# Another order of the head, a band mask on VectorE, narrow blank matmuls and one stay for x, in an attention and gated-MLP kernel

## The chip, the cores and the metric

The kernel runs on one core of one Trainium2 chip. A core has TensorE (PE; its weight loads are a row of their own, PEld), VectorE (DVE), ScalarE (ACT), GpSimd (POOL), SyncE (SP, which issues DMAs) and 16 DMA engines. The metric is device time in microseconds of one execution; the time before is the median of three runs.

## The reference

Two stages, f32 in and out. Attention over 4 batches, 8 heads, 768 positions, 64 dimensions; each query sees the keys less than 16 positions away and one summary key for each block of 32 (the maximum of the block's keys, with the mean of its values):

```python
k_sum = k.reshape(B, H, nb, block, D).max(axis=3)
v_sum = v.reshape(B, H, nb, block, D).mean(axis=3)
mask_l = np.abs(pos[:, None] - pos[None, :]) < window
scores_s = scale * np.einsum('bhsd,bhnd->bhsn', q, k_sum) + np.log(block)
a = softmax(concat([np.where(mask_l, scores_l, -1e9), scores_s]))
x = a @ concat([v, v_sum])
...
h = x @ w_in                        # 3072 x 512 by 512 x 2048
g = h * (1.0 / (1.0 + np.exp(-beta * h)))
out = g @ w_out                     # by 2048 x 512
```

## The kernel before

**Tiles.** The four batches run one after the other. A batch has four pairs of heads, g = 0 to 3 (128 partitions hold two heads of 64), and two halves of 384 positions, u = 0 and 1. For each pair, `kT[g]` and `qn[g]` hold keys and queries turned by TensorE, `km[g]` the block maxima, `vst[g]` V as loaded (f32) and `ve[:, g]`, `vo[:, g]` its bf16 casts at two alignments. `e` is a pair's and half's exponentials, `xn` the attention result, `xT` the same turned, 4 x 128 rows, `h_sb` the gated MLP activations. PSUM is held as `one[0]`, `one[1]` (one bank each) and `big[0..2]` (two banks each); in the steps below a bank number x below 6 is half of `big[x // 2]`, 6 and 7 are `one[0]` and `one[1]`.

**The order.** All engines run in order of the program (the schedule is written by hand). Batch 0's first part is the list HEAD, one step for each entry: `kt`/`qt` turn k and q of a pair into a bank (16 transposes, L384), `kc`/`qc` copy them out on the engine named (a = ACT, d = DVE, p = POOL), `km` the block maxima, `vc` the cast of V, `vu`/`vl` copies from ve to vo, `sm`/`mc` the block means of V and their copy into `vm_one`, `sc` scores of (pair, half, big), `ex` their exponential on ACT, `av` the weighted sum of the first half, `no` its division (DVE), `xt`/`xc` the turn of x, `wi` a load of 512 columns of w_in, `begin` the first h matmuls, `blank` matmuls on zeros, `silu` the load of ScalarE's table.

**Scores.** In batch 0, `scores0` sums three things in PSUM: the summary keys (L415, 2 matmuls), the 96 keys around each tile of 64 queries (L422, 12 matmuls), and -30000 where the band ends, as matmuls of the identity with `off` (L417, 2 matmuls, 384 wide) and of `edge` (L426, 2 matmuls) at the first or last tile. Later batches instead multiply the exponentials by a 0/1 `mask` on DVE (`mask_e`, L451).

**After the head.** `main` holds TensorE's steps: eight `h_two` (two h tiles each of the first half, L578), sixteen `h_half` of the second half (L584), then output and the next batches. The table AT gives side steps a place in it: a step with place p follows main step number floor(p), so 1.99 stands behind the second h_two. Among them: `first` (`v_odd`, POOL copies, and `vm_rest`, four DVE copies of block means for two pairs, L480), `loads` (`more_loads`: k of batch 1, four parts of w_out, q of batch 1), `av0` (AV of the second halves of two pairs, 24 matmuls, and their norms), `x0` (x of the second halves of two pairs: six transposes and a DVE copy), `scale` (w_out by 1/beta on DVE, L337), `clear` (zeros in `kw` and `more_masks`, which makes `mask`), `kt` (k of batch 1).

**Queues of loads.** GpSimd issues the casting loads (f32 to bf16: k and q as rows, w_in, w_out) on one queue, in its own program order, between its casts and copies. SP issues V. `HOLD` puts V of pair 1 behind the third load of k, so pairs 1 to 3 of V start when k is in. In the head GpSimd's order is: loads of k and q, cast of V of pair 0, cast of pair 1 (it waits for that load), w_in part 0, two copies, w_in part 1, cast of pair 3 in two pieces, w_in parts 2 and 3.

Of the kernel before, what the change touches and what calls it, by code (L numbers as in the profile page):

```python
# [12 lines left out]
    'first': [-2.097, 0.853, -1.457, 0.459, 0.237, 1.035, 1.122, 1.113],  # L13
    'loads': [2.306],
    'av0': [1.99, 4.754],
    'x0': [5.759, 6.564],
    'scale': [8.171, 16.158, 16.833, 21.634],
    'clear': [6.428, 6.644],
# [84 lines left out]
def kernel(  # L103
# [190 lines left out]
    def more_masks():  # L294
        nc.vector.tensor_copy(out=mask[:], in_=band[:, None, :].to_broadcast([P, NT, QT]))
# [34 lines left out]
    def load_w_in(lo, hi):  # L330
        return nc.gpsimd.dma_start(out=w_in_sb[:, :, lo:hi], in_=w_in_r[:, :, lo:hi])
# [72 lines left out]
    def q_tile(g, h, m):  # L404
        return qn[g][h * D:(h + 1) * D, m * QT:(m + 1) * QT]
# [565 lines left out]
```

## Time and profile before

| | |
|---|---|
| three runs | 209.53, 209.86, 211.06 us; median 209.86 |
| the profiled execution | 210.59 us, span 208.9 us |
| TensorE, DVE, ACT, POOL busy | 96%, 66%, 60%, 29% of the span |
| first h matmul (L578) | 25.84 us |
| first h matmul of the second halves (L584) | 38.30 us |
| DMA queues | GpSimd's casting loads 22.0% of 16 engines' span, SP's and others' 54.9% and 8.8% |

The span runs from the first to the last instruction; the execution's own time has 1.69 us more around it. The chain of waits follows the last instruction back to what released it. A timeline's row has start, length, engine, line, operation, output and inputs, count, and in brackets the idle time before it with what ended it. Rows of several instructions overlap with their neighbours, since TensorE's matmuls are pipelined. A windows row gives the busy time of each engine within a stretch, then the clock granted to TensorE, the DMA engines' share and their GB/s.

### The profile page before, as it was taken

The page shows a single profiled execution, that of the slowest core. Times are in us where ns is not written, and L with a number is a line of the kernel's source. Part 1 is how long each engine was busy: PE and PEld are TensorE (multiplying, and loading weights), DVE is VectorE, ACT ScalarE, POOL GpSimd, SP SyncE. Part 2 cuts the span into 40 slices and gives each one's busy share as a digit, 9 for nine tenths or more (in the row PEclk, how much of TensorE's full clock was granted, in tenths as well). Part 3 has the DMA queues.
Part 4 walks back from the last instruction along what each step waited for, and adds up shares of the span by engine and source line. Part 5 has one row for each costly group of instructions (what it writes and reads, how often), then busy time and mean ns, then how long its engine had stood idle before and what let it go on. Part 6 is the DMA issues. An engine that isn't in the chain of part 4 may idle for free.

```text
span 208.9 us, 5772 instructions
## 1 busy us (share of the span) xinstructions
PE 200.0 (96%) x2383; PEld 138.9 (67%) x2387; DVE 138.8 (66%) x314; ACT 124.9 (60%) x189; POOL 61.5 (29%) x95
## 2 busy tenths in 40 slices
PE   7887899999999999999999999999999999999993
PEld 2476666665555675666888975667888856668882
DVE  4496674599999982868999621999889304464132
ACT  2365876679678212966979238768894439662210
POOL 7706991101530017422520162452501100000011
PEclk9999999999999999999999999999999999999998
DMA  5997999999958999999779979999936820000242
GB/s 114 188 221 124 167 208 207 206 207 222 184 139 222 218 246 260 225 188 209 148 173 250 199 213 285 205 192 202 122 126 66 189 100 3 0 0 3 100 100 100
DMA packets 79193, 34.12 MB, mean 163 GB/s; under 512 B 61488, under 2 KB 76224, under 8 KB 79168
## 3 DMA queue, kind: packets, MB, share of 16 engines
q1 hardware_dynamic: 61968, 23.92, 54.9%
q0 software_dynamic: 7424, 7.34, 22.0%
q10 hardware_dynamic: 9776, 2.50, 8.8%
q8 instruction: 18, 0.29, 0.6%
q14 instruction: 7, 0.06, 0.1%
HBM read 27.37 MB, written 6.29 MB: 161 GB/s over the span
## 4 chain that ended last, share of the span: by engine, by line
PE 78%; DMA 10%; DVE 6%; issue 2%; ACT 2%; POOL 1%; POOLq 0%
PE big L600 28%; PE one L664 16%; PE acc L664 12%; PE big L578 5%; DMA vst<-in_v_dram 4%; DMA w_in_sb<-in_moe_w_in_dram 4%; PE one L584 3%; DMA krow<-in_k_dram 3%; PE one L615 3%; PE one L600 2%; PE big L436 2%; PE big L511 2%; PE big L584 2%; PE big L384 1%; DVE xn L538 1%
## 5 line engine op out<-in xcount | busy, mean ns | idle before, releaser
L600 PE MATMUL big<-xT,w_in_sb 128*128 128x384 bf16 x360 | 60.5, 326 | 0.0
L600 PEld LDWEIGHTS <-w_in_sb 128*128 128x128 bf16 x384 | 37.6, 98 | 25.1 <-issue 0.7
L611 ACT ACTIVATE h_sb<-big,beta_sb 128x768 bf16<-128x768 f32 x45 | 39.6, 905 | 24.0 <-PE big L600 23.9
L664 PEld LDWEIGHTS <-h_sb 128*128 128x128 bf16 x320 | 30.6, 98 | 4.6 <-issue 0.2
L645 POOL TENSOR_TENSOR o_sb<-p,u 128x256 f32<-128x256 f32 x10 | 7.3, 728 | 84.8 <-DVE u L645 74.4
L447 ACT ACTIVATE e<-big,bias 128x768 bf16<-128x768 f32 x32 | 27.4, 900 | 6.7 <-PE big L426 4.3
L664 PE MATMUL one<-w_out_sb,h_sb 128*128 128x256 bf16 x240 | 30.4, 273 | 0.2 <-DVE u L645 0.2
L664 PEld LDWEIGHTS <-s_sb 128*128 128x128 bf16 x240 | 23.1, 98 | 3.3 <-issue 0.5
L645 DVE TENSOR_TENSOR s_sb<-h_sb 128x768 bf16<-128x768 bf16 (+2 forms) x16 | 7.8, 488 | 23.7 <-ACT h_sb L611 23.6
L645 DVE TENSOR_TENSOR u<-one,p 128x256 f32<-128x256 f32 x20 | 8.4, 419 | 17.4 <-PE one L664 17.4
L456 POOL CAST ve<-vst 128x832 bf16<-128x832 f32 (+2 forms) x16 | 14.5, 914 | 17.9 <-DMA vst<-in_v_dram 14.9
L615 PE MATMUL one<-w_out_sb,h_sb 128*128 128x512 bf16 x61 | 14.5, 380 | 0.4 <-issue 0.3
L451 DVE TENSOR_TENSOR e<-e,mask 128x768 bf16<-128x768 bf16 x24 | 14.1, 618 | 0.4 <-ACT e L447 0.2
L368 ACT COPY o_sb<-one 128x256 f32<-128x256 f32 (+1 forms) x14 | 6.1, 433 | 12.9 <-PE one L664 7.1
L365 POOL COPY kw<-km 128x288 bf16<-128x288 bf16 x12 | 6.4, 534 | 22.5 <-DVE km L357 12.2
L361 DVE TENSOR_REDUCE km<-kT 128x24 bf16<-128x768 bf16 x12 | 11.3, 944 | 2.1 <-ACT kT L368 2.1
L538 DVE TENSOR_TENSOR xn<-big,r 128x768 bf16<-128x768 f32 x12 | 11.5, 957 | 0.4
L578 PE MATMUL big<-xT,w_in_sb 128*128 128x384 bf16 x64 | 11.4, 326 | 0.3 <-DMA w_in_sb<-in_moe_w_in_dram 0.3
L664 PE MATMUL acc<-t_sb,h_sb 128*128 128x256 bf16 x80 | 10.9, 273 | 0.0
L368 ACT COPY p<-acc 128x256 f32<-128x256 f32 x10 | 3.8, 376 | 11.6 <-PE acc L664 7.3
L664 PE MATMUL one<-t_sb,s_sb 128*128 128x256 bf16 x80 | 10.4, 273 | 0.2 <-ACT o_sb L368 0.2
L831 ACT ACTIVATE h_sb<-big,beta_sb 128x384 bf16<-128x384 f32 x16 | 8.3, 578 | 3.7 <-PE big L578 3.7
(145 smaller groups left out, 315.0 us busy)
## 6 DMA issues: line engine op xcount, KB each, us to landing
out_dram<-o_sb SPq DMA_DIRECT2D x19, 256.0 KB, 3.5
vst<-in_v_dram SPq DMA_DIRECT2D x13, 336.0 KB, 5.2
kst<-in_k_dram SPq DMA_DIRECT2D x8, 384.0 KB, 4.8
qst<-in_q_dram SPq DMA_DIRECT2D x8, 384.0 KB, 4.5
w_in_sb<-in_moe_w_in_dram POOLq DMA_DIRECT2D x4, 512.0 KB, 8.9
w_out_sb<-in_moe_w_out_dram POOLq DMA_DIRECT2D x4, 512.0 KB, 14.2
vo<-ve SPq DMA_DIRECT2D x12, 107.2 KB, 2.6
vst<-in_v_dram SPq DMA_DIRECT2D x3, 416.0 KB, 8.9
```

The source lines that it names most:

```text
L361: nc.vector.tensor_reduce(out=km[g][:, NK:NK + nb], in_=kT[g][:, W:W + S].rearrange("p (n f) -> p n f", f=block), op=ALU.max, axis=AX.X)
L447: nc.scalar.activation(out=e[:], in_=s[:, :, 0:HS], func=ACTF.Exp, bias=bias[:, 0:1], scale=scale)
L451: nc.vector.tensor_mul(out=e.rearrange("p h (m q) -> p h m q", q=QT), in0=e.rearrange("p h (m q) -> p h m q", q=QT), in1=(mask2 if b > 1 e ...
L456: eng.tensor_copy(out=ve[:, g, lo:hi, 0:D], in_=vst[g][:, lo:hi])
L538: nc.vector.tensor_mul(out=x[:, 3 * us[0]:3 * us[0] + 3 * n].rearrange("p (k j) h d -> p k (j h) d", k=n), in0=tv[:, :, :, 0:D], in1=r[:, ...
L578: nc.tensor.matmul(t[:, 0:HS], w_in_sb[:, ki, i * P:(i + 1) * P], xT[:, ki, 0:HS], start=(ki == 0), stop=(ki == k1 - 1))
L584: nc.tensor.matmul(t[:, 0:HS], w_in_sb[:, ki, i * P:(i + 1) * P], xT[:, ki, lo:lo + HS], start=(ki == 0), stop=(ki == k1 - 1))
L600: nc.tensor.matmul(o, w_in_sb[:, ki, i * P:(i + 1) * P], x, start=(ki == 0), stop=(ki == k1 - 1))
L611: nc.scalar.activation(out=o, in_=t, func=ACTF.Silu, scale=beta_sb[:, i:i + 1])
L615: nc.tensor.matmul(t[:, 0:hi - lo], h_sb[:, n, ms * P:(ms + 1) * P], w_out_sb[:, n, lo:hi], start=(n == 0), stop=(n == k2 - 1))
L645: eng.tensor_tensor(out=o, in0=a, in1=b, op=op)
L664: nc.tensor.matmul(SLOTS[n], a[:, j, t * P:(t + 1) * P], b[:, j], start=(j == 0 and n not in (2, 3, 7)), stop=(j == J2 - 1), skip_group_ch ...
```

## The change

Five things change; the rest of the kernel and its arithmetic in later batches stay.

1. HEAD has another order, other banks and other engines for some copies. `blank` of 4 and of 2 matmuls, 512 wide, become 27 each of 64 wide (a single 512-wide one follows later). Both halves' scores of a pair stand near each other. `wi` 0 and 1 stand earlier in the list, and part 0 is issued as two loads of two 128-row chunks each.
2. The second halves' scores lose the `off` and `edge` matmuls; `mask_e(0, g, 1)` on DVE multiplies their exponentials by the mask instead, in four new side steps `mk0`.
3. For that, `more_masks` is a step of the head (`mask`), its row of ones moves from GpSimd's `mask` to DVE's `band`, and it leaves `clear`.
4. The side steps move: `av0` from 1.99 and 4.754 to 2.99 and 5.4, `vm_rest` of pairs 2 and 3 from about 1.1 to 3.5 and 3.6.
5. `x0` moves from 5.759 and 6.564 to 6.4 and 6.41: both turns of x behind the same h_two.

```diff
 AT = {
-    'first': [-2.097, 0.853, -1.457, 0.459, 0.237, 1.035, 1.122, 1.113],
+    'first': [-2.097, -1.9, -1.457, 0.459, 0.12, 0.13, 3.5, 3.6],
-    'av0': [1.99, 4.754],
-    'x0': [5.759, 6.564],
+    'av0': [2.99, 5.4],
+    'x0': [6.4, 6.41],
-    'clear': [6.428, 6.644],
+    'clear': [6.428],
+    'mk0': [0.2, 0.3, 3.7, 3.8],
...
 HEAD = [
-    ('blank', 10, 512), ('beta',), ('blank', 2, 512), ('kt', 0, 3), ('blank', 4, 512), ('kc', 0, 'a'), ('kt', 1, 6),
+    ('blank', 10, 512), ('beta',), ('blank', 2, 512), ('kt', 0, 3), ('blank', 27, 64), ('kc', 0, 'a'), ('kt', 1, 6),
...
+    ('sc', 2, 1, 1), ('wi', 2), ('ex', 2, 0), ('no', 1), ('vl', 3, 'd'), ('vl', 2, 'a'), ('mc', 2, 'a'), ('xt', 1, 5),
...
     def more_masks():
+        nc.vector.memset(band[NK:NK + nb], 1.0)
         nc.vector.tensor_copy(out=mask[:], in_=band[:, None, :].to_broadcast([P, NT, QT]))
...
-        nc.gpsimd.affine_select(out=mask[:, NT - 1], in_=mask[:, NT - 1], compare_op=ALU.is_ge, fill=0.0,
+        nc.gpsimd.affine_select(out=mask[0:NK, NT - 1], in_=mask[0:NK, NT - 1], compare_op=ALU.is_ge, fill=0.0,
                                 base=QT + W - 1, pattern=[[0, QT]], channel_multiplier=-1)
-        nc.gpsimd.memset(mask[NK:NK + nb], 1.0)
...
     def scores0(g, u, bg):
         s = big[bg]
+        edges = u == 0
...
-        for h, r in enumerate(H2):
+        for h, r in enumerate(H2 if edges else ()):
             nc.tensor.matmul(s[0:NK, h, 0:HS], off[r, h * QT:h * QT + NK],
...
-        for h, r in enumerate(H2):
+        for h, r in enumerate(H2 if edges else ()):
             c = u * (HT - 1) * QT
             nc.tensor.matmul(s[:, h, c:c + QT], edge[r, u], identity[r, r], start=False, stop=True)
...
     def w_in_part(i):
-        x = load_w_in(512 * i, 512 * i + 512)
+        x = load_w_in(512 * i, 512 * i + 512, 0, k1 // 2 if i == 0 else k1)
+        if i == 0:
+            load_w_in(0, 512, k1 // 2, k1)
...
-    at("clear", [clear_kw, more_masks])
+    at("clear", [clear_kw])
+    at("mk0", [lambda g=g: mask_e(0, g, 1) for g in range(G)])
```

GpSimd's queue in the head, from the cast of V of pair 1 (`vst1`) on. Before:

```order
L456 CAST ve_120<-vst1_92 128x13x64 [waits DMAHW3_49,Pool_49]
L331 DMA w_in_sb_183<-in_moe_w_in_dram 128x4x512 [waits DMASW0_49]
L374 COPY vo_121<-ve_120 32x2x3x64 [waits Pool_49]
L374 COPY vo_121<-ve_120 64x2x3x64
L331 DMA w_in_sb_183<-in_moe_w_in_dram 128x4x512
L456 CAST ve_120<-vst3_94 128x7x64 [waits DMAHW5_49,Pool_49]
L456 CAST ve_120<-vst3_94 128x6x64
```

After (lines of the changed kernel):

```order
L458 CAST ve_120<-vst1_92 128x13x64 [waits DMAHW3_49,Pool_49]
L332 DMA w_in_sb_183<-in_moe_w_in_dram 128x2x512 [waits DMASW0_49]
L332 DMA w_in_sb_183<-in_moe_w_in_dram 128x2x512
L332 DMA w_in_sb_183<-in_moe_w_in_dram 128x4x512
L458 CAST ve_120<-vst2_93 128x13x64 [waits DMAHW4_49]
L375 COPY vo_121<-ve_120 64x2x3x64 [waits Pool_49]
L458 CAST ve_120<-vst3_94 128x7x64 [waits DMAHW5_49,Pool_49]
```

The first load of w_in stands behind the same cast; the second now follows it with nothing between, and the cast of pair 2 has come to this queue (half of pair 3's has left it).

DVE's queue behind the head, from the copies of block means on (`e_415`, `e_474` are the second halves' exponentials of pairs 0 and 1, `r` and `xn` their norms). Before:

```order
L480 COPY ve_120<-vm_one_122 32x2x3x64
L537 RECIPROCAL r_725<-one0_78 128x6 [waits PE_49,Activation_49]
L538 TENSOR_TENSOR xn_420<-one0_78,r_725 128x384 [waits DVE_49]
L537 RECIPROCAL r_728<-one1_79 128x6 [waits PE_49]
L538 TENSOR_TENSOR xn_519<-one1_79,r_728 128x384 [waits DVE_49]
```

After:

```order
L482 COPY ve_120<-vm_one_122 32x2x3x64 [waits Pool_49]
L453 TENSOR_TENSOR e_415<-e_415,mask_111 128x768
L453 TENSOR_TENSOR e_474<-e_474,mask_111 128x768
L539 RECIPROCAL r_785<-one0_78 128x6 [waits PE_49,Activation_49]
L540 TENSOR_TENSOR xn_574<-one0_78,r_785 128x384 [waits DVE_49]
L539 RECIPROCAL r_788<-one1_79 128x6 [waits PE_49]
L540 TENSOR_TENSOR xn_630<-one1_79,r_788 128x384 [waits DVE_49]
```

Two masks stand between the copies of two pairs' means and the norms; the other two pairs' copies and masks follow behind these norms.

More of the change, by code (lines that the diff above doesn't have):

```diff
@@ L84 @@
 HEAD = [
[12 rows of a table removed]
[11 rows of a table added]
+    ('begin', 0, 2, 3), ('begin', 1, 0, 3), ('silu',),
 ]
@@ L329, with load_w_in @@
     w_out_r = moe_w_out.rearrange("(a p) n -> p a n", p=P)
-    def load_w_in(lo, hi):
-        return nc.gpsimd.dma_start(out=w_in_sb[:, :, lo:hi], in_=w_in_r[:, :, lo:hi])
+    def load_w_in(lo, hi, a=0, b=k1):
+        return nc.gpsimd.dma_start(out=w_in_sb[:, a:b, lo:hi], in_=w_in_r[:, a:b, lo:hi])
     def load_w_out(i, n=4):
@@ L412, in scores0 @@
         s = big[bg]
+        edges = u == 0
         H2 = [slice(h * D, (h + 1) * D) for h in range(2)]
         for h, r in enumerate(H2):
-            nc.tensor.matmul(s[:, h, 0:HS], km[g][r], qn[g][r, u * HS:(u + 1) * HS], start=True, stop=False)
-        for h, r in enumerate(H2):
+            nc.tensor.matmul(s[:, h, 0:HS], km[g][r], qn[g][r, u * HS:(u + 1) * HS], start=True, stop=not edges)
+        for h, r in enumerate(H2 if edges else ()):
             nc.tensor.matmul(s[0:NK, h, 0:HS], off[r, h * QT:h * QT + NK],
@@ L422, in scores0 @@
                 nc.tensor.matmul(s[0:NK, h, j * QT:(j + 1) * QT], kT[g][r, m * QT:m * QT + NK],
-                                 q_tile(g, h, m), start=False, stop=False)
-        for h, r in enumerate(H2):
+                                 q_tile(g, h, m), start=False, stop=not edges, skip_group_check=True)
+        for h, r in enumerate(H2 if edges else ()):
             c = u * (HT - 1) * QT
@@ L820 @@
             "qt": turn0("q", qrow), "qc": q_copy, "sm": means, "mc": means_copy, "sc": scores0,
-            "ex": lambda g, u: weigh(0, g, u), "vc": lambda g, e, lo=0, hi=JV: v_cast(eng_of(e), g, lo, hi),
+            "ex": lambda g, u: weigh(0, g, u), "mask": more_masks, "vc": lambda g, e, lo=0, hi=JV: v_cast(eng_of(e), g, lo, hi),
             "vu": upper, "vl": lower, "av": av0, "no": lambda g: norm(0, g, turns.pop(("o", g)), [0]),
```

20 rows, old and new, of the table HEAD are left out of this document.

## The prediction, made before the changed kernel ran

> **What bounds the kernel now.** I read the page's first part, then the chain of waits up to 80 us, then each engine's timeline over the first 40 us, and last the bytes that the DMA engines move in each microsecond there. Two lines of the page's first part first.
>
> ```profile
> span 208.9 us, 5772 instructions
> PE 200.0 (96%) x2383; PEld 138.9 (67%) x2387; DVE 138.8 (66%) x314; ACT 124.9 (60%) x189; POOL 61.5 (29%) x95
> ```
>
> TensorE has 8.9 us without work in the whole span, so a change of the head can win only what TensorE waits there, or what it does there for nothing. The chain of waits says what the head waits for (start, length, what):
>
> ```profile
> 3.36 6.06 DMA krow<-in_k_dram
> 9.44 7.76 DMA vst<-in_v_dram
> 17.32 0.82 POOL ve L456
> 18.14 7.65 DMA w_in_sb<-in_moe_w_in_dram
> 25.84 0.82 PE big L578 x4
> ...
> 38.46 0.65 PE one L584 x4
> ...
> 58.51 0.91 ACT e L447
> ...
> 59.44 1.58 DVE e L451 x2
> ```
>
> So the head isn't TensorE's: k's third row load ends, the load of V of pair 1 held behind it lands, GpSimd casts that, and only then issues w_in, whose first part lands at 25.8. The first h matmul (L578) starts on it. From there TensorE is almost never idle. But DVE is full as well, from 39.85 on:
>
> ```profile
> 39.85 1.14 DVE L337 TENSOR_SCALAR w_out_sb<-w_out_sb,inv_beta 128x512 bf16<-128x512 bf16 x4 [1.68 <-DMA w_out_sb<-in_moe_w_out_dram]
> ...
> 39.90:58.00 18.10, 18.03 (x205) 10.38 (x204) 18.07 (x33) 13.90 (x23) 3.85 (x7) 1.00 1.15 204
> 58.00:76.00 18.00, 17.29 (x276) 10.88 (x278) 17.07 (x33) 9.11 (x15) 1.87 (x2) 1.00 0.98 191
> ```
>
> The windows' numbers are length, then busy time of PE, PEld, DVE, ACT and POOL, then clock, DMA share and GB/s. Between 39.90 and 58.00 TensorE works 18.03 of 18.10 us and DVE 18.07. DVE's row of work starts when the first part of w_out lands (its 1.68 us of waiting say so) and runs into the masks of batch 1 at 59.44. Hence two chains must both become earlier: TensorE's, from the first h matmul, and the DMA stream that ends in w_out. The end moves by the smaller of the two gains.
>
> **The change part by part.** GpSimd's issues first.
>
> ```profile
> 17.32 0.88 POOL L456 CAST ve<-vst 128x832 bf16<-128x832 f32 x1 [7.95 <-DMA vst<-in_v_dram]
> 18.14 0.76 POOL L331 DMA_DIRECT2D w_in_sb<-in_moe_w_in_dram  x1
> 18.94 1.05 POOL L374 COPY vo<-ve 32x384 bf16<-32x384 bf16 x2
> 19.93 0.74 POOL L331 DMA_DIRECT2D w_in_sb<-in_moe_w_in_dram  x1
> 20.72 1.01 POOL L456 CAST ve<-vst 128x448 bf16<-128x448 f32 x2
> 21.67 1.48 POOL L331 DMA_DIRECT2D w_in_sb<-in_moe_w_in_dram  x2
> ```
>
> In the list of steps w_in moves far ahead, but on GpSimd's queue the cast of pair 1 still stands before it, and what that cast waits for (vst at 17.2) isn't touched: the first issue stays at 18.14. After it come three issues in a row (two halves of part 0, then part 1): 18.14 + 3 x 0.75 = 20.4, then the cast of pair 2 (0.88, until now on DVE), a 0.50 copy and half of pair 3's cast (0.50): 22.3. The last two parts follow at 22.3 and 23.0 instead of 21.67 and 22.4; the stream has work until then (two parts of 512 KB at some 200 GB/s, from 20.25 to 25.4). The mask's select on GpSimd and pair 0's copy (0.50) run in its 7.95 us of waiting: nothing.
>
> What the stream can win stands in its windows:
>
> ```profile
> 20.00:21.00 1.00, 0.98 (x23) 0.73 (x23) 0.85 (x3) 0.98 (x3) 0.96 (x2) 1.00 0.69 109
> 22.00:23.00 1.00, 0.87 (x30) 0.73 (x27) 0.32 (x2) 0.95 (x2) 1.00 (x2) 1.00 1.25 179
> 23.00:24.00 1.00, 0.74 (x20) 0.63 (x21) 0.80 (x4) 0.82 (x2) 0.90 (x3) 1.00 0.81 74
> 24.00:25.00 1.00, 1.00 (x32) 0.83 (x30) 0.71 (x2) 0.33 (x1) 0.90 (x3) 1.00 1.13 181
> 40.00:45.00 5.00, 5.00 (x59) 3.11 (x58) 5.00 (x11) 3.07 (x7) 0.00 (x0) 1.00 1.25 210
> ```
>
> Against the 205 to 210 GB/s of the full stream, 22 to 25 us lack 26 + 131 + 24 of 205, or 0.9 us: a hole between the first part of w_in and the second, which was issued 1.8 us after it. Issued 0.75 us after the one before it, the second should close it. I take 0.75 us (the ends: 0.9, and below nothing 0.75 lost, if every transfer on this queue pays such a start and there is now one more). Then w_out's first part lands near 39.1, and DVE's row starts 0.75 earlier.
>
> TensorE's chain. A score step shows what the second halves lose (first rows of the pieces of one step):
>
> ```profile
> 18.80 0.34 PE L415 MATMUL big<-qn,km 64*128 64x384 bf16 x2
> 18.97 0.33 PE L417 MATMUL big<-identity,off 64*96 64x384 bf16 x2
> 19.14 0.42 PE L422 MATMUL big<-qn,kT 64*96 64x64 bf16 x12
> 19.39 0.19 PE L426 MATMUL big<-identity,edge 64*128 64x64 bf16 x2
> 19.52 0.27 PE L519 MATMUL one<-vm_one,e 128*128 128x65 bf16 x3
> ...
> 17.50 0.23 PE L422 MATMUL big<-qn,kT 64*96 64x64 bf16 x2 [1.32 <-issue]
> ...
> 22.30 0.57 PE L473 MATMUL one<-ve,A_avg 128*32 128x128 bf16 x14
> ...
> 14.87 0.36 PE L519 MATMUL one<-vm_one,e 128*128 128x65 bf16 x6
> 15.16 0.22 PE L525 MATMUL one<-ve,e 96*64 96x65 bf16 x1
> ```
>
> The step takes 0.72; without L417 (0.17) and L426 (0.13) 0.42. Four such steps: 1.2 us of TensorE gone, but most of it in a stage that waits for vst anyway (1.32 us of standing up to 17.50). What counts is the tail behind the sums of pairs 2 and 3, which need pair 3's cast: 22.30 now, 22.3 then. Behind them come sums 0.57, scores 0.42, x 0.17, AV 0.60, x 0.17, AV 0.60 and x 0.17, together 2.70, with about 0.3 of waits for DVE's norm of pair 2 as the last x needs it: the first h matmuls at 25.3 instead of 25.84. Part 0's first half, 256 of 512 KB, is there by then: 1.3 us less to move at 200 GB/s, so 24.5 where the whole part lands at 25.8. So 0.55 us.
>
> Behind that nothing is added to TensorE: the same 64 matmuls L578, 48 of AV, 12 transposes of x. Moving the second halves' x into one stay saves at most the small waits; 0 taken, 0.3 as the upper end. AV of the second halves now waits for the masks. Their price:
>
> ```profile
> 57.70 3.32 DVE L451 TENSOR_TENSOR e<-e,mask 128x768 bf16<-128x768 bf16 x4
> ...
> 65.77 1.03 DVE L451 TENSOR_TENSOR e<-e,mask 128x768 bf16<-128x768 bf16 x2
> ...
> 27.32 0.35 DVE L480 COPY vo<-vm_one 32x384 bf16<-32x384 bf16 x1
> ...
> 29.23 0.25 DVE L480 COPY ve<-vm_one 32x384 bf16<-32x384 bf16 x1
> ```
>
> A mask costs 0.52 to 0.83. DVE is done with the norms at 25.9; four of the eight copies of the means (27.32 to 29.48 now, so 1.1 for four) and two masks (1.0 to 1.7) end by 28.7, and AV of pairs 0 and 1, one h tile later than before, starts at 29.4. The second two masks end near 33.7, AV of pairs 2 and 3 starts at 33.9: just covered, 0.1 lost at worst; without the cover each mask costs TensorE its full 0.8. The mask's making (0.35, from 37.67 to the head) lies before kc of pairs 2 and 3, while TensorE waits for vst anyway: nothing.
>
> The 54 narrow blanks: the 128-row, 65-wide matmuls L519 follow each other at 0.048 us (six between 14.87 and 15.16), so 27 take 1.3 us against 0.97 and 0.4 of four and two wide ones. The transposes of k for pairs 1 to 3 come 0.3 to 0.5 later; 5 us lie between them and the wait for vst: nothing.
>
> The sum: TensorE 0.55 earlier, the stream 0.75 earlier, so the end 0.55 earlier. The profiled execution took 210.59 us with a span of 208.9; it gives 210.04. It lay 0.73 above the median of 209.86, to which I apply the same 0.55: 209.3 us.
>
> **The rivals.** The hole stays. DVE works from 19.30 to 20.32 on a cast between SBUF tiles while GpSimd writes the second part's request (19.93), and in the new order DVE copies V of pair 1 (19.1 to 20.0) beside the issue at 19.6. If such DVE work holds the request back, the hole is there again, w_out lands at 39.85 as before, and DVE's full row takes back what TensorE won: 209.8. Against it: the four issues last 740 to 759 ns alike, beside DVE or not. The Trainium skill, page "SBUF — State Buffer", section "Who interferes with whom", says that a DVE copy between SBUF tiles in a two-port mode locks GpSimd out, so that a GpSimd DMA starves for descriptors; the equal durations neither show it nor exclude it, and by that rule the sum is this rival's.
>
> One more start. The split makes five transfers of four. If the hole is a price of each start on a queue that has little in it, there are two holes of 0.75, one more than now: w_out lands at 40.6 and DVE's full row starts as much later: 210.6, slower. For it: the hole has the form of the first start (20 to 21 us, 109 GB/s). Against it: no later boundary in the stream shows one.
>
> A cold TensorE. Its work thins out: from 17 to 22.3 us stand sums 0.5, scores 0.42 and 0.72 and AV 0.6, or 2.2 us, where there were 3.6 (sums, three whole score steps, AV, two x), and the wide blanks become narrow.
>
> ```profile
> 1.27 4.45 PE L737 MATMUL one<-blank 128*128 128x512 bf16 x10 [1.27 <-DVE blank L232]
> 7.09 1.04 PE L737 MATMUL one<-blank 128*128 128x512 bf16 x4
> 16.00:17.00 1.00, 0.18 (x8) 0.11 (x5) 1.00 (x2) 0.00 (x0) 0.00 (x0) 1.00 1.27 237
> ```
>
> The first ten blanks took 0.44 each, later ones 0.24: about 4.4 us at half speed until it runs fast. Should that come again when h begins, 4.4 us of matmuls cost 2.2 more: 211.5. It decides only if the thin stage counts as idle; the 1.3 us of standing at 16 to 17 us did not slow the matmuls behind it. The Trainium skill, "TensorE: Matmul & The Clock Gate", section "HAM oscillation — how this bites in real kernels", asks for a gap of about 3.4 us; no single gap here is half of that, so its rule lowers this rival's chance.
>
> **How the numbers follow.** My forecast (the hole closes) has 0.48, its own range 208.9 to 209.7. The hole stays: 0.28. One more start: 0.12. Cold TensorE: 0.05. The rest, 0.07, is a gain beyond the forecast, with the full 0.85 of stream and waits or more. I take 208.4 to 210.8, which holds the first three and the spread of the runs before, and leaves out the cold case and both ends. A measurement of this kernel tells about 1% (2.1 us) from no change; every case but the cold one and part of the rest lies within it: faster 0.05, same 0.88, slower 0.07.
>
> **What would show it.** The hole: no microsecond from 21 to 26 under 150 GB/s, and the wait of DVE for w_out ending near 39.1. TensorE: first h matmul at 25.3, first L584 matmul (second halves) near 37.8. Masks: no wait of AV for the masks over 0.2. I am wrong if the first issue of w_in moves from 18.14, if TensorE's matmuls in h are spaced by more than 0.17, or if DVE's row between 40 and 58 shortens although nothing in it is changed.

## The result, and the profile after

The changed kernel takes 211.01 us (median of 20 runs, 209.91 to 212.49), the kernel before 209.98 (median of 20 runs, 209.01 to 211.83). The ratio is 1.0051, with a 95% interval of 1.0031 to 1.0071: 0.5% slower and just above the range of 208.4 to 210.8, where a gain of 0.55 us was forecast. The profiled execution took 211.23 us with a span of 209.4 (before: 210.59 and 208.9).

First the chain of waits of the changed kernel, from the landing of k to batch 1 (start, length, what):

```profile
10.37 6.24 DMA vst<-in_v_dram
16.73 0.88 POOL ve L458
17.61 2.12 POOL w_in_sb L332 x3
19.73 0.89 POOL ve L458
20.69 0.58 POOL vo L375
21.33 0.57 POOL ve L458
21.94 0.55 PE one L475 x13
25.40 1.28 PE big L580 x4
27.00 3.43 PE big L580 x20
...
38.81 0.65 PE one L586 x4
...
59.85 1.63 DVE e L453 x2
...
83.73 15.76 PE big L602 x96
```

Before, the chain went from the cast of V of pair 1 through the landing of w_in to the first h matmuls (L578). Now it goes through GpSimd's own row: the cast, three requests (2.12 us), two more casts with a copy between them, and then TensorE's sums of pairs 2 and 3 (L475). The h matmuls (now L580) begin earlier, at 25.19 instead of 25.84; of that 0.59 us is an earlier landing of V in this execution (its cast starts at 16.73 instead of 17.32). But the first four take 1.28 us, where four took 0.65 elsewhere, and the h matmuls of the second halves (now L586) come at 38.81 instead of 38.46, the second pair of masks of batch 1 at 59.85 instead of 59.44, the 96 h matmuls of batch 1 (now L602) at 83.73 instead of 83.16. Hence 0.35 of the 0.57 us seen at 83.73 has arisen by 40 us.

TensorE's clock in single microseconds (third number from the end; it was 1.00 in each of these microseconds before), and, from TensorE's timeline, what stood ahead:

```profile
21.00:22.00 1.00, 0.06 (x3) 0.06 (x4) 0.64 (x3) 0.42 (x1) 0.94 (x3) 1.00 1.23 191
23.00:24.00 1.00, 1.00 (x27) 0.91 (x26) 0.53 (x2) 0.97 (x2) 0.90 (x3) 0.91 1.15 185
24.00:25.00 1.00, 1.00 (x22) 0.84 (x20) 0.58 (x2) 0.48 (x1) 0.93 (x2) 0.50 1.20 196
27.00:28.00 1.00, 1.00 (x7) 0.56 (x6) 0.97 (x3) 0.95 (x2) 0.94 (x2) 0.88 1.24 209
```

```profile
20.69 0.23 PE L475 MATMUL one<-ve,A_avg 128*32 128x128 bf16 x1 [0.33 <-DVE xn L540]
21.94 0.55 PE L475 MATMUL one<-ve,A_avg 128*32 128x128 bf16 x13 [1.02 <-POOL ve L458]
```

TensorE waits 0.33 us for the norm of pair 0 and 1.02 for GpSimd's cast of pair 3. It works 0.06 of the microsecond at 21. Two us later its clock is half, until 27.2: 3.4 us, in which about 1.7 us of work is lost.

The loads, in longer stretches (the last number is GB/s), before and then after:

```profile
20.00:24.00 4.00, 3.59 (x88) 2.86 (x88) 2.90 (x9) 3.72 (x6) 3.85 (x7) 1.00 0.98 139
30.00:37.00 7.00, 7.00 (x74) 4.47 (x71) 3.28 (x20) 4.84 (x11) 2.05 (x3) 1.00 1.24 207
```

```profile
20.00:24.00 4.00, 2.65 (x67) 2.12 (x66) 2.76 (x9) 2.81 (x6) 3.77 (x7) 0.98 1.11 161
30.00:37.00 7.00, 7.00 (x89) 4.34 (x88) 4.77 (x14) 5.13 (x11) 2.69 (x4) 1.00 1.13 171
```

The hole at 23 to 24 us is gone, but 20 to 24 us move 161 GB/s, not 205, and a second hole has opened: 30 to 37 us move 171 instead of 207. That costs 7 x 36 / 207 = 1.2 us of the full stream. What is loaded there was requested later, by GpSimd's timeline (before at 27.51 and 28.29), and w_out lands hardly sooner than before, by DVE's:

```profile
27.46 0.72 POOL L466 COPY vo<-ve 32x384 bf16<-32x384 bf16 x1
28.13 0.79 POOL L196 DMA_DIRECT2D krow<-in_k_dram  x1
28.91 2.99 POOL L335 DMA_DIRECT2D w_out_sb<-in_moe_w_out_dram  x4
```

```profile
27.07 1.52 DVE L453 TENSOR_TENSOR e<-e,mask 128x768 bf16<-128x768 bf16 x2
33.32 1.03 DVE L453 TENSOR_TENSOR e<-e,mask 128x768 bf16<-128x768 bf16 x2
39.72 1.14 DVE L338 TENSOR_SCALAR w_out_sb<-w_out_sb,inv_beta 128x512 bf16<-128x512 bf16 x4 [1.13 <-DMA w_out_sb<-in_moe_w_out_dram]
```

So there were three suspects, all of them new: the half clock, the masks on DVE (two pairs at 27.07 and 33.32, beside the loads that thin out), and the requests (w_in's part 0 in two, k and w_out later).

### The profile page after: what moved, and what is told of

Same layout as the page of the kernel before. It is cut to its first block, busy times and chain, and to the rows that moved or that the text cites. A ratio compares the mean times of both kernels' runs of the same rounds, so it can differ in the third digit from the quotient of the medians.

```text
span 209.4 us, 5848 instructions
## 1 busy us (share of the span) xinstructions
PE 201.4 (96%) x2420; PEld 140.2 (67%) x2420; DVE 139.9 (67%) x318; ACT 124.9 (60%) x191; POOL 63.7 (30%) x94
## 4 chain that ended last, share of the span: by engine, by line
PE 81%; DMA 6%; DVE 5%; POOL 3%; ACT 2%; issue 1%; ACTq 0%; POOLq 0%; DVEq 0%
PE big L602 28%; PE one L666 17%; PE acc L666 13%; PE big L580 5%; PE one L586 3%; DMA krow<-in_k_dram 3%; DMA vst<-in_v_dram 3%; PE one L617 3%; PE one L602 2%; PE big L438 2%; PE big L513 2%; PE big L586 2%; PE big L385 2%; DVE e L453 1%; ACT e L449 1%
## 5 line engine op out<-in xcount | busy, mean ns | idle before, releaser
L602 PE MATMUL big<-xT,w_in_sb 128*128 128x384 bf16 x360 | 60.5, 326 | 0.0
L602 PEld LDWEIGHTS <-w_in_sb 128*128 128x128 bf16 x384 | 37.6, 98 | 25.0 <-issue 0.7
L449 ACT ACTIVATE e<-big,bias 128x768 bf16<-128x768 f32 x32 | 27.2, 899 | 3.3 <-PE big L438 1.2
L647 DVE TENSOR_TENSOR s_sb<-h_sb 128x768 bf16<-128x768 bf16 (+2 forms) x16 | 8.8, 553 | 24.0 <-ACT h_sb L613 24.0
L458 POOL CAST ve<-vst 128x832 bf16<-128x832 f32 (+1 forms) x16 | 14.4, 908 | 13.1 <-DMA vst<-in_v_dram 7.9
L453 DVE TENSOR_TENSOR e<-e,mask 128x768 bf16<-128x768 bf16 x28 | 17.0, 635 | 1.3 <-ACT e L449 1.0
L366 POOL COPY kw<-km 128x288 bf16<-128x288 bf16 x12 | 7.4, 620 | 28.5 <-DVE km L358 18.6
L617 PE MATMUL one<-w_out_sb,h_sb 128*128 128x512 bf16 x64 | 15.0, 380 | 0.0
L540 DVE TENSOR_TENSOR xn<-big,r 128x768 bf16<-128x768 f32 (+1 forms) x13 | 12.0, 927 | 0.4
L580 PE MATMUL big<-xT,w_in_sb 128*128 128x384 bf16 x64 | 12.1, 343 | 0.0
L570 POOL CAST qn<-qst 128x768 bf16<-128x768 f32 x8 | 8.2, 1034 | 9.9 <-DMA qst<-in_q_dram 5.9
L666 PE MATMUL acc<-t_sb,s_sb 128*128 128x256 bf16 x80 | 10.4, 273 | 0.0
```

The costliest lines, as they stand in the source:

```text
L449: nc.scalar.activation(out=e[:], in_=s[:, :, 0:HS], func=ACTF.Exp, bias=bias[:, 0:1], scale=scale)
L453: nc.vector.tensor_mul(out=e.rearrange("p h (m q) -> p h m q", q=QT), in0=e.rearrange("p h (m q) -> p h m q", q=QT), in1=(mask2 if b > 1 e ...
L458: eng.tensor_copy(out=ve[:, g, lo:hi, 0:D], in_=vst[g][:, lo:hi])
L540: nc.vector.tensor_mul(out=x[:, 3 * us[0]:3 * us[0] + 3 * n].rearrange("p (k j) h d -> p k (j h) d", k=n), in0=tv[:, :, :, 0:D], in1=r[:, ...
L580: nc.tensor.matmul(t[:, 0:HS], w_in_sb[:, ki, i * P:(i + 1) * P], xT[:, ki, 0:HS], start=(ki == 0), stop=(ki == k1 - 1))
L602: nc.tensor.matmul(o, w_in_sb[:, ki, i * P:(i + 1) * P], x, start=(ki == 0), stop=(ki == k1 - 1))
```

## The experiments

In what follows the stream is the row of GpSimd's casting loads, and the dip is its thin stretch from 30 to 37 us.

All are the changed kernel or the kernel before with one or two edits. Each was run 12 times beside the kernel before, whose medians were 210.06, 210.14, 210.24 and 210.20 in the four groups of four. The column "20 to 24" and "30 to 37" are the loads' GB/s in the profiled execution, "asked" the start of the request for k of batch 1, "h, half 2" the first h matmul of the second halves there.

| run | median us | ratio to before, 95% interval | 20 to 24 | asked | 30 to 37 | h, half 2 |
|---|---|---|---|---|---|---|
| before (20 runs) | 209.98 | 1 | 139 | 27.51 | 207 | 38.30 |
| changed (20 runs) | 211.01 | 1.0051 [1.0031, 1.0071] | 161 | 28.13 | 171 | 38.64 |
| fill | 211.26 | 1.0052 [1.0021, 1.0084] | 139 | 28.11 | 177 | 37.35 |
| v3first | 211.11 | 1.0046 [1.0010, 1.0082] | 177 | 28.01 | 173 | 36.44 |
| nomask | 210.30 | 1.0018 [0.9988, 1.0048] | 133 | 27.64 | 203 | 37.30 |
| oldhead | 210.67 | 1.0025 [0.9990, 1.0061] | 158 | 26.37 | 202 | 37.18 |
| early | 210.10 | 0.9996 [0.9966, 1.0025] | 168 | 25.18 | 206 | 38.48 |
| nomask_late | 210.92 | 1.0053 [1.0026, 1.0079] | 160 | 28.42 | 181 | 36.84 |
| v3early | 209.93 | 0.9988 [0.9959, 1.0018] | 164 | 24.94 | 206 | 36.60 |
| row | 209.95 | 1.0001 [0.9972, 1.0029] | 206 | 26.61 | 176 | 37.55 |
| after_early | 210.68 | 1.0025 [0.9995, 1.0055] | 172 | 24.95 | 206 | 38.10 |
| v3early_whole | 209.40 | 0.9979 [0.9951, 1.0007] | 206 | 24.48 | 205 | 37.22 |
| row_early | 210.19 | 1.0012 [0.9987, 1.0036] | 204 | 24.22 | 203 | 37.84 |
| row_split | 210.46 | 1.0021 [0.9991, 1.0050] | 167 | 26.29 | 207 | 37.34 |
| after_whole | 209.83 | 0.9973 [0.9942, 1.0005] | 204 | 26.84 | 177 | 37.11 |
| after_early_whole | 209.37 | 0.9950 [0.9920, 0.9980] | 208 | 24.49 | 202 | 36.63 |
| early_whole | 209.99 | 0.9978 [0.9945, 1.0011] | 205 | 24.09 | 204 | 36.83 |
| v3_noblank | 210.18 | 0.9971 [0.9934, 1.0007] | 207 | 24.66 | 205 | 38.90 |

The ratio is an estimate with its interval and not the quotient of the two medians; in v3_noblank, whose runs fall into two clusters, they differ most. A difference of two medians under some 0.5 us is not told apart by 12 runs; the columns of the profile are each of one execution. When the load of V of pair 1 lands moves them too: its cast began between 15.31 and 17.32 us, for no reason that an edit gives.

### First group: clock or masks

`fill`, blanks in TensorE's wait:

```diff
-('sm', 7, 2, 3),
+('blank', 5, 512), ('sm', 7, 2, 3),
```

> The changed kernel with five 512-wide blank matmuls where TensorE stands from 20.7 to 21.9 us, before the sums of pairs 2 and 3. Cold theory (the standing makes the clock fall to half for 3.4 us, and that is what costs): clock 1.00 from 20 to 30 us, first h matmul near 24.7 instead of 25.4, first h matmul of the second halves near 37.5 instead of 38.8, median 0.8 to 1.3 us under the changed kernel's 211.0, so 209.7 to 210.2. Stream theory (the loads that end in w_out and DVE's row behind them set the end, and the clock costs nothing there): clock 1.00 too, but w_out lands near 39.7 as before and the median stays at 210.8 to 211.2.

Measured: 211.26 us, clock 1.00 from 20 to 40 us, the second halves' h at 37.35, 1.3 us earlier than in the changed kernel. But w_out lands at 40.11, and TensorE loses what it had won (windows of fill, then DVE's row):

```profile
40.00:58.00 18.00, 16.60 (x197) 9.64 (x195) 17.59 (x33) 13.03 (x22) 5.06 (x6) 1.00 1.17 200
```

```profile
40.11 1.14 DVE L338 TENSOR_SCALAR w_out_sb<-w_out_sb,inv_beta 128x512 bf16<-128x512 bf16 x4 [2.82 <-DMA w_out_sb<-in_moe_w_out_dram]
```

TensorE works 16.60 of 18 us from 40 to 58, where it was full (17.93) before; 1.4 us of that is one wait for q of batch 1, the last of the casting loads. The cold theory falls as an account of the end: with the clock repaired the loads take the gain back.

`v3first`, pair 3's cast before pair 2's copy on GpSimd:

```diff
-('sc', 1, 1, 1), ('vu', 2, 'p'), ('ex', 1, 0),
+('sc', 1, 1, 1), ('ex', 1, 0),
...
-('vc', 3, 'p', 0, 7),
+('vc', 3, 'p', 0, 7), ('vu', 2, 'p'),
```

> The changed kernel with GpSimd's cast of V of pair 3 ahead of its copy for pair 2: the sums of pairs 2 and 3 can start near 21.3 instead of 21.9, and TensorE stands about 1.0 instead of 1.6 us. Cold theory: if 1.0 us is short enough, the clock stays at 1.00 and h begins 1.3 us earlier, median 209.5 to 210.0; if not, the clock still falls for 3.4 us, h begins 0.6 earlier and the median is 210.4. Stream theory: no change at the end, 210.8 to 211.2.

Measured: 211.11. The second halves' h at 36.44 is 1.9 us earlier than in the kernel before, and the end isn't: ahead of the turn of q of batch 1, at 51.15 us, TensorE waits 1.3 us for DVE's scaling of w_out, whose first part landed only at 39.59. The stream theory's number.

`nomask`, the mask back on TensorE:

```diff
-        edges = u == 0
+        edges = True
...
-    at("mk0", [lambda g=g: mask_e(0, g, 1) for g in range(G)])
```

> The changed kernel with the mask of the second halves back on TensorE (the matmuls of off and edge for both halves) and no masks on DVE. Mask theory (the masks on DVE slow the loads beside them, 30 to 37 us at 131 to 185 GB/s, and with them w_out): no dip there, w_out lands near 38.6, median 210.0. Cold theory: the clock falls as in the changed kernel, up to 0.3 us more TensorE work ahead of h, median 211.0 to 211.5.

Measured: 210.30, no dip, w_out at 39.02. This fits the mask theory. But there is another difference: k was requested at 27.64, not 28.13, and the loads were further behind (133 GB/s from 20 to 24 us). Of these 0.49 us, 0.32 come from an earlier V load and at most 0.17 from copies on GpSimd that no mask holds up. The half clock is missing from this profile as well, so nomask alone doesn't separate the three suspects.

`oldhead`, the kernel before's HEAD in the changed kernel:

```diff
 HEAD = [
-    ('blank', 10, 512), ('beta',), ('blank', 2, 512), ('kt', 0, 3), ('blank', 27, 64), ('kc', 0, 'a'), ('kt', 1, 6),
+    ('blank', 10, 512), ('beta',), ('blank', 2, 512), ('kt', 0, 3), ('blank', 4, 512), ('kc', 0, 'a'), ('kt', 1, 6),
...
-    ('kc', 1, 'a'), ('blank', 27, 64), ('km', 0), ('kt', 2, 5), ('vc', 0, 'p'), ('kt', 3, 0), ('km', 1), ('mask',),
+    ('kc', 1, 'a'), ('blank', 2, 512), ('km', 0), ('km', 1), ('mask',), ('vc', 0, 'p'), ('vl', 0, 'p'), ('kt', 2, 7), ('kc', 2, 'd'),
```

> The changed kernel with the list HEAD of the kernel before (only the mask's making added to it; the wide blanks are back too, since they stand in the list), all else as changed: masks on DVE, side steps at their new places, w_in part 0 in two loads. Cold theory: clock 1.00 throughout the head, first h matmul near 25.5, median 209.5 to 210.0, at or under the kernel before. If the side steps, the masks or the split load are to blame: 210.8 to 211.3 at clock 1.00.

Measured: 210.67, between the two, and its clock was half from 11.6 to 15.0 us, in another place. Masks on DVE and no deep dip: against the mask theory. It left open what is slow in it; the split, below, is one part that it shares with the changed kernel.

### Second group: when the loads are requested

What separates the profiles with a dip from those without is how late k was asked for, seen from where the stream stood. `early` is fill with the requests moved and nothing else:

```diff
-    'loads': [2.306],
+    'loads': [-1.8],
```

> The run with five blanks (fill) and one thing more: k of batch 1, the four parts of w_out and q of batch 1 are requested before GpSimd's copies of pairs 2 and 3, so near 25.6 us instead of 28.1; the masks stay on DVE. Late-request theory (the stream runs dry at 30 to 37 us because k of batch 1 and w_out are requested only 2 to 3 us before the last part of w_in has landed): no stretch from 30 to 37 us under 195 GB/s, w_out lands near 38.6 instead of 40.1, h of batch 1 starts near 82.6 instead of 84.1, median 209.6 to 210.1. Mask theory (the masks on DVE slow the loads): the dip stays at 170 to 180 GB/s in the mean of 30 to 37 us, and the median at 211.0 to 211.4.

Measured: 210.10, 1.16 us under fill. GpSimd's requests, DVE's masks beside them, and the loads (timeline twice, then windows):

```profile
25.18 0.79 POOL L196 DMA_DIRECT2D krow<-in_k_dram  x1
25.95 3.00 POOL L335 DMA_DIRECT2D w_out_sb<-in_moe_w_out_dram  x4
```

```profile
27.75 1.03 DVE L453 TENSOR_TENSOR e<-e,mask 128x768 bf16<-128x768 bf16 x2
```

```profile
30.00:37.00 7.00, 7.00 (x91) 4.47 (x90) 4.62 (x14) 5.32 (x11) 1.79 (x4) 1.00 1.24 206
```

The masks are there, the dip isn't. h began late in this execution (its load of q ended at 11.44, and the clock was half from 12 to 15.4), so it doesn't show the 82.6 that was expected for h of batch 1.

`nomask_late`, from nomask, one repeated copy of pair 3 ahead of the requests:

```diff
+    'wait': [2.3],
...
+    at("wait", [lambda: v_odd(nc.gpsimd, 3, 3, 6)])
```

> The run with the masks back on TensorE (nomask) and one thing more: GpSimd copies pair 3 a second time (same values) ahead of the loads, so that k of batch 1 is requested near 28.7 us instead of 27.6. Late-request theory: the dip is there without any mask, 170 to 185 GB/s in the mean of 30 to 37 us against 203 in nomask, w_out lands 1 us later, near 40.0, median 210.9 to 211.3. Mask theory: no dip, w_out near 39.0, median at 210.2 to 210.5.

Measured: 210.92, 0.62 over nomask. No mask runs on DVE, and the dip is there (windows of nomask, then of nomask_late in half microseconds at its deepest):

```profile
30.00:37.00 7.00, 7.00 (x74) 4.49 (x72) 4.78 (x19) 4.78 (x10) 2.22 (x3) 1.00 1.23 203
```

```profile
30.00:37.00 7.00, 7.00 (x73) 4.47 (x71) 4.31 (x23) 4.44 (x9) 3.01 (x4) 1.00 1.18 181
30.50:31.00 0.50, 0.50 (x5) 0.29 (x3) 0.49 (x4) 0.44 (x1) 0.50 (x2) 1.00 1.00 76
```

Masks without a dip, a dip without masks: the mask theory falls, and the time of the request is shown as the cause of the dip. What the dip costs at the end is less sure: the intervals of nomask and nomask_late overlap, and w_out, expected near 40.0, landed at 38.99, as in nomask (39.02), in an execution whose V load came 0.33 us sooner. The gap begins at 30.0, 1.6 us behind the start of the request at 28.42.

`v3early`: v3first with `('blank', 2, 512)` ahead of `('sm', 7, 2, 3)` and `'loads': [-1.8]`.

> The run v3first (cast of pair 3 ahead of the copy for pair 2) with two blanks in what is left of TensorE's wait and the early requests of the run early. Late-request theory: both gains hold, h at 24.0, first h of the second halves near 36.5, w_out near 37.8 and no dip, h of batch 1 near 82.0, median 209.0 to 209.6, under the kernel before. Mask theory: dip as in v3first (173 GB/s), median 210.8 to 211.2.

Measured: 209.93, not the 209.0 to 209.6 that was expected, though h of the second halves came at 36.60 and 30 to 37 us moved 206 GB/s. Its waits of TensorE (total, count, longest) say where the rest went:

```profile
PE big L385 <- DMA qrow<-in_q_dram: 1.3, 1, 1.3
```

q of batch 1 is the last of the casting loads. TensorE is ahead of the whole stream, so only a denser stream moves the end. The thin stretch left is 20 to 24 us.

`row`, the hole of the kernel before closed alone:

```diff
-('wi', 0), ('ex', 0, 1), ('vl', 1, 'p'),
+('wi', 0), ('wi', 1), ('ex', 0, 1), ('vl', 1, 'p'),
...
-('vl', 2, 'd'), ('wi', 1), ('vc', 3, 'p', 0, 7),
+('vl', 2, 'd'), ('vc', 3, 'p', 0, 7),
```

> The kernel before with the second part of w_in requested directly behind the first, ahead of two GpSimd copies; nothing else. Late-request theory: the hole at 23 to 24 us (74 GB/s) closes, w_out lands 0.5 to 0.8 earlier (39.1 to 39.4), a smaller dip near 31 us gives back a part; TensorE's chain stays, so the end moves by 0 to 0.5: median 209.6 to 210.0. If the hole isn't set by the time of the request: the hole stays and the median is 210.0.

Measured: 209.95, no difference from before (interval 0.9972 to 1.0029). Its loads, two stretches:

```profile
20.00:24.00 4.00, 3.59 (x88) 2.82 (x88) 2.67 (x10) 3.38 (x6) 3.80 (x8) 1.00 1.24 206
30.00:37.00 7.00, 7.00 (x73) 4.50 (x72) 2.96 (x20) 5.07 (x10) 1.17 (x2) 1.00 1.16 176
```

The hole is closed, at 206 GB/s and not at 161 as in the changed kernel, and part of the gain goes into a dip. There is no mask on DVE in this kernel either.

### Third group: the split

`row_split` adds to row the changed kernel's two loads for part 0:

```diff
-        x = load_w_in(512 * i, 512 * i + 512)
+        x = load_w_in(512 * i, 512 * i + 512, 0, k1 // 2 if i == 0 else k1)
+        if i == 0:
+            load_w_in(0, 512, k1 // 2, k1)
```

> The run row with part 0 of w_in in two loads as in the changed kernel; nothing else. Split theory: 20 to 24 us fall from 206 to 160 to 175 GB/s, w_out lands 0.4 to 0.8 later than in row, median 210.0 to 210.4. If the thin start of the changed kernel comes from its other work (copies on DVE beside GpSimd's requests): 20 to 24 us stay above 195 GB/s and the median at 209.95.

Measured: 210.46, and

```profile
20.00:24.00 4.00, 3.61 (x92) 2.94 (x91) 2.95 (x9) 2.90 (x5) 3.80 (x8) 1.00 1.14 167
30.00:37.00 7.00, 7.00 (x73) 4.47 (x71) 3.27 (x20) 5.03 (x10) 0.85 (x2) 1.00 1.24 207
```

20 to 24 us fall from 206 to 167 GB/s, as the split theory has it. The dip behind it is gone, since the stream stands further back when k is asked for. So w_out, which was to land 0.4 to 0.8 later than in row (38.39), landed at 37.60, in an execution whose V load came 0.8 us sooner: in row's order the split and the dip cancel out, and the two medians aren't told apart. DVE's cast of V, a copy between SBUF tiles, starts at 18.38, behind the three requests (16.13 to 18.30), so the thin stretch needs no such work on DVE beside the requests.

`v3early_whole` takes the split out of v3early:

```diff
-        x = load_w_in(512 * i, 512 * i + 512, 0, k1 // 2 if i == 0 else k1)
-        if i == 0:
-            load_w_in(0, 512, k1 // 2, k1)
+        x = load_w_in(512 * i, 512 * i + 512, 0, k1)
```

> The run v3early with part 0 of w_in in one load again instead of two. Split theory (one more start thins the stream while it fills): 190 to 206 GB/s in the mean of 20 to 24 us instead of 164, w_out lands near 37.6 and q of batch 1 0.6 to 0.8 earlier, so TensorE's 1.3 us of waiting for q at 50 us shrinks by as much; h of batch 1 near 82.5, median 209.2 to 209.5. If the split costs nothing: 164 GB/s stays and the median is 209.8 to 210.1.

Measured: 209.40, 0.53 under v3early (the intervals overlap); 206 GB/s from 20 to 24 us, TensorE's wait for q gone, 17.98 of 18 us busy from 40 to 58. As the split theory has it.

`after_early`: the changed kernel with `'loads': [-1.8]` alone.

> The changed kernel with the early requests alone (k of batch 1, w_out and q of batch 1 ahead of GpSimd's copies of pairs 2 and 3), without the five blanks. Late-request theory: no dip from 30 to 37 us, median 0.6 to 1.1 under the changed kernel's 211.0, so 209.9 to 210.4. Cold theory, now that the loads are not late: the granted clock falls to 0.5 for 3.4 us in more of its runs than in the run early, and it costs 0.4 to 0.8 us against early (210.1), so 210.5 to 210.9.

Measured: 210.68. No dip (206 GB/s), but the gain against the changed kernel's 211.01 is 0.33, less than the late-request theory had and within what the cold theory had; the stream's thin start and the clock (half from 23.3 to 26.7 us in its profile) are still there.

`row_early`: row with `'loads': [-1.8]` and the copies of pairs 0 and 1 ahead of them.

> The run row (kernel before, first two parts of w_in requested in a row) with the early requests: GpSimd's copies of pairs 0 and 1, then k of batch 1, w_out and q of batch 1, then the copies of pairs 2 and 3. Late-request theory: no dip at 29.5 to 35 us (176 GB/s in row), w_out lands near 37.4. If the kernel before is bound by TensorE behind 38 us, the end stays: 209.7 to 210.0. If it is bound by the loads as the changed kernel is: 209.0 to 209.4.

Measured: 210.19. The loads are full (204 and 203 GB/s), w_out has landed at 37.64, and the end stays: the kernel before is bound by TensorE behind 38 us. A full stream alone is worth nothing, a faster TensorE alone is worth nothing (v3first); it takes both.

### Fourth group: dividing the loss

`after_whole`: the changed kernel with part 0 in one load, and nothing else (the diff of v3early_whole).

> The changed kernel with part 0 of w_in in one load again; nothing else. Three-part theory (split, late requests and clock each cost a piece, and the loads are the bound): 20 to 24 us near 205 GB/s, but the last part of w_in then lands earlier and k of batch 1 is still requested near 28, so the dip from 30 to 37 us deepens, and the median only falls to 210.5 to 211.0. If the split is the whole cause: 209.9 to 210.2, as the kernel before.

Measured: 209.83, 1.2 us under the changed kernel, more than either theory had. Its loads, GpSimd's cast of pair 3 and request for k, and TensorE's waits ahead of the sums:

```profile
20.00:24.00 4.00, 2.96 (x70) 2.23 (x68) 3.82 (x11) 2.84 (x6) 3.72 (x8) 1.00 1.24 204
30.00:37.00 7.00, 7.00 (x73) 4.51 (x72) 5.71 (x27) 4.71 (x10) 1.40 (x2) 1.00 1.17 177
```

```profile
20.23 0.56 POOL L458 CAST ve<-vst 128x448 bf16<-128x448 f32 x1
26.84 0.79 POOL L196 DMA_DIRECT2D krow<-in_k_dram  x1
```

```profile
20.33 0.19 PE L527 MATMUL one<-vo,e 96*64 96x65 bf16 x1 [0.32 <-DVE vo L372]
21.15 0.28 PE L475 MATMUL one<-ve,A_avg 128*32 128x128 bf16 x3 [0.47 <-DVE xn L540]
21.68 0.50 PE L475 MATMUL one<-ve,A_avg 128*32 128x128 bf16 x11 [0.25 <-DVE ve L458]
```

One request less takes 0.75 us out of GpSimd's row. So the cast of pair 3 starts at 20.23 instead of 21.33 (0.36 of it from an earlier V load), TensorE stands 0.25 us for pair 3 instead of 1.02 (in all 1.04 us ahead of the sums instead of 1.35), the clock stays at 1.00 in this profile, and k is asked for at 26.84 instead of 28.13 (again with 0.36 from the V load). The dip stays, as expected, because the stream is earlier by as much. The split costs three times: in the stream, on GpSimd's row, and by that on TensorE.

`after_early_whole`: split undone and `'loads': [-1.8]`.

> The changed kernel with part 0 of w_in in one load and the early requests, so without either hole in the loads, but with TensorE's stand before the sums of pairs 2 and 3. Three-part theory: no stretch from 20 to 40 us under 195 GB/s, the clock still falls to 0.5 for 3.4 us in most runs, median 209.9 to 210.4, 0.3 to 0.6 above early_whole.

Measured: 209.37, ratio 0.9950 with an interval of 0.9920 to 0.9980: faster than the kernel before by 0.8 us and than the changed kernel by 1.6. The clock stayed at 1.00 in its profile, against what was expected.

```profile
20.00:24.00 4.00, 3.39 (x82) 2.46 (x78) 3.79 (x11) 2.99 (x6) 3.75 (x7) 1.00 1.24 208
30.00:37.00 7.00, 7.00 (x73) 4.50 (x72) 5.46 (x25) 4.40 (x10) 1.26 (x3) 1.00 1.23 202
40.00:58.00 18.00, 17.98 (x216) 10.23 (x210) 17.73 (x31) 14.15 (x23) 7.01 (x8) 1.00 1.10 196
```

`early_whole`: the same with fill's five blanks.

> As after_early_whole, with the five blanks of fill in TensorE's stand. Three-part theory: loads full from 20 to 40 us, clock 1.00 in most runs, median 209.4 to 209.9: what the change was good for, without its three costs. If a part of the loss lies elsewhere (masks on DVE, places of AV and x): 210.3 or more.

Measured: 209.99, just above the 209.4 to 209.9 that was expected. The blanks win nothing where the stand is already short; whether they cost the 0.6 us between the two medians, 12 runs don't settle (the intervals overlap).

`v3_noblank`: v3early_whole without its two blanks.

> The run v3early_whole without its two blanks: GpSimd casts pair 3 ahead of its copy for pair 2, so that TensorE stands for about 1.0 us instead of 1.6. If such a stand is short enough, the clock stays and the median is that of v3early_whole, 209.2 to 209.6; if not, the clock falls in most runs and the median is 209.7 to 210.1.

Measured: 210.18, and its profile shows the half clock from 22.3 to 25.8 us, behind a stand of 0.88 and 0.47 us:

```profile
21.18 0.19 PE L527 MATMUL one<-vo,e 96*64 96x65 bf16 x1 [0.88 <-DVE vo L372]
21.99 1.02 PE L475 MATMUL one<-ve,A_avg 128*32 128x128 bf16 x14 [0.47 <-DVE xn L540]
```

```profile
20.00:24.00 4.00, 2.65 (x47) 1.84 (x44) 3.54 (x9) 2.06 (x6) 3.82 (x7) 0.79 1.23 207
```

So with full loads the clock does count. In the twelve runs of this kernel, the five with a mean clock of 0.992 or less have a median of 210.54, the other seven 209.26. Over the 140 runs of the kernel before beside these groups it is 210.69 (53 runs) and 209.74 (87 runs), about 1 us. (A mean of 0.992 is one stretch of 3.4 us at half speed: 3.4 x 0.5 / 209 = 0.008.) In the changed kernel it is 13 of 20 runs, 211.13 against 210.76: half speed is more frequent there and costs less, which fits loads that are late as well. The mean doesn't tell where in the head a run was slow: two profiles (oldhead and early) had it at 11 to 16 us.

The same count shows that TensorE's stand brings the half clock on. Four pairs of kernels differ only in wide blanks that fill the stand: changed and fill, after_early and early, after_early_whole and early_whole, v3_noblank and v3early_whole. Without the blanks 13 of 20, 6, 3 and 5 of 12 runs have a mean clock of 0.992 or less, together 27 of 56; with them 2, 2, 2 and none of 12, together 6 of 48.

## Why the prediction was wrong

**The bound.** Right: two chains, TensorE's and the casting loads', and the end moves by the smaller gain. v3first (TensorE alone, 1.9 us by 36 us, nothing at the end), row_early (loads alone, nothing) and after_early_whole (both, 0.8) show it. So the gain that was forecast was there to be had, and the changed kernel's way of requesting its loads took it away.

**The first request of w_in** was to stay at 18.14, and came at 17.56, by the landing of V, which moves by itself and was luck. The form was right: three requests in a row of 0.73 us, the cast of pair 3 ending at 21.89 against a forecast of 22.3.

**"Issued 0.75 us after the one before it, the second should close it."** This step failed. It holds for two whole loads (row: 206 GB/s). With part 0 in two loads, 20 to 24 us run at 133 to 177 GB/s in all ten profiles with the split, and at 204 to 208 in all seven with whole loads requested in a row. The text had priced the split at 0.75 us in the rival "one more start", by the form of the first start, and gave it a chance of 0.12 because no later boundary showed such a price. That an extra transfer thins the stream, as this rival had it, is shown: it holds too when the GB/s are taken from 2 to 6 us behind each run's own first request of w_in (121 to 166 with the split, 185 to 191 without). Its form is not: w_out was to land at 40.6 and landed at 39.72, so that its time, 210.6, the nearest to 211.0 of all that were named, is partly luck. The split's other price was not seen: it is one request more, 0.75 us on GpSimd, ahead of the cast for which TensorE waits and of all later requests. The forecast had counted the 0.75 us on GpSimd's row, and called it nothing, because the stream had work until then.

The rival "the hole stays" (0.28), in which a cast on DVE holds a request back, is not what thinned the stream: row_split is thin with no such cast beside its three requests.

**"The last two parts follow at 22.3 and 23.0 ...; the stream has work until then."** True of w_in, but the count ended there. k of batch 1 and w_out, behind it on the same row, were asked for 0.62 us later (28.13 for 27.51) by a stream that was to be 0.75 us earlier. The dip at 30 to 37 us (1.2 us) is what came of it, shown by early and nomask_late.

**TensorE's chain.** First h at 25.3 forecast, 25.19 measured: the number was right by luck in part. From the cast of pair 1 to first h it is 8.46 us, 8.52 before, so that the gain is V's earlier landing; in fill, where the clock stays up, it is 8.07, so 0.45 less, near the 0.55 us that was forecast. That the first h of the second halves follows 12.5 us later was not: it came at 38.64 instead of 37.8, by the half clock. The rival "a cold TensorE" (0.05) was right in its mechanism, with a size of 3.4 us instead of 4.4 at half speed. But it doesn't explain the time: without it (fill) the kernel took 211.26. The argument against it was that the 1.3 us of standing at 16 to 17 us hadn't slowed anything, and this argument is unsafe: stands of 1.35 us (0.33 and 1.02) here and in v3_noblank (0.88 and 0.47) were followed by half speed, and filling the stand made it rare (6 of 48 runs against 27 of 56). The Trainium skill, "TensorE: Matmul & The Clock Gate", section "HAM oscillation — how this bites in real kernels", asks for an idle gap above about 3.4 us. The traces disagree: the longest single wait here was 1.02 us. They agree with the length of its window, 3.4 us, as the time that the half speed lasts.

**The masks on DVE** were costed at nothing, rightly: AV waited for no mask, and early has the masks and no dip. The masks do hold up GpSimd's copies (0.72 us beside a mask, 0.50 in the kernel before), and these stand ahead of the requests, but this is at most 0.17 us of nomask's earlier request. The rest of nomask's gain isn't divided. Nor do the masks hold the requests themselves back: in early the four requests of w_out take 3.00 us beside DVE's masks, in the kernel before 2.98 without any. The Trainium skill, "SBUF — State Buffer", section "Who interferes with whom", says that a DVE instruction with two SBUF inputs contends with GpSimd instructions that read SBUF; the longer copies agree. It has a GpSimd DMA starve beside DVE work in a two-port mode and says that `tensor_tensor`, the masks' instruction, has no such mode; the requests in early agree.

**The narrow blanks** took 0.96 us per 27 (from 7.28 in the profile after) instead of 1.3, and like the single stay of x they show in no wait: nothing, as forecast.

**What stays open.** Why a load split in two thins the stream, though it asks for the same bytes: the runs show that it does, not how. Whether the hole of the kernel before came of the late request or of DVE's cast beside it (19.30 to 20.32, the request at 19.93): row moved the request away from both. When a stand of some 1.3 us halves the clock: before it stood as long at 16 to 17 us and did not. And why the end keeps less than was won at 38 us: from the second halves' h to the h of batch 1 it is 39.9 us in after_early_whole and 39.7 in the changed kernel, 39.5 before, and a wait of TensorE for ACT's `o_sb` of 0.8 to 1.1 us at 70 to 73 us, 0.2 before, stands there. No run takes it out.

## What to carry to other kernels

When a queue of loads is made denser at one place, follow it to its last request: each request behind it must also come earlier, or the hole only moves. An extra request is paid by everything behind it on the engine that issues it, so count the casts and the requests there before halving a load for an early start. And where two chains are both full, measure each gain together with the other's: alone neither shows.

## What the runs showed of the hardware

- In the six profiles with a dip the stream thins 1.6 to 2.9 us behind the start of the request for the next casting load: 76 GB/s at 30.5 us with the request at 28.42 (nomask_late), 104 at 29.5 with the request at 26.61 (row). With the request at 25.18 (early) there is none. The stream then stayed under its 205 GB/s for 2 us (nomask_late) to 7 us (the changed kernel).
- One 512 KB load in place of two of 256 KB at the head of the queue: 204 to 208 GB/s against 133 to 177 from 20 to 24 us.
- TensorE's clock fell to half for about 3.4 us behind waits of 1.35 us in all within 2 us, and not behind all such waits. With blanks in the wait, 6 of 48 runs show such a fall in their mean clock, without them 27 of 56.
